# Routed attention followed by a gated MLP: the second maxima step's mask moved beside the scores in 32-row tiles

## The chip, the cores and the metric

The kernel runs on one core of a Trainium2 chip. The metric is the device time of one execution in microseconds (us); lower is better. Before the change the median of three runs is 1022.64 us (1022.56 to 1022.86).

## The reference

```python
B, H, S, D = 4, 8, 768, 64          # 16 clusters
q_assign = argmax(q_n @ c_n.T); k_assign = argmax(k_n @ c_n.T)      # per head, rows normalised
mask = q_assign[:, :, :, None] == k_assign[:, :, None, :]
scores = where(mask, (q @ k.T) / sqrt(D), -1e9)
attn = softmax(scores)               # less the row's maximum, sum + 1e-9
x = (attn @ v) laid out as (B*S, H*D) = (3072, 512)
h = x @ w_in                         # w_in (512, 2048)
g = h * erf(softplus(h))
out = g @ w_out                      # w_out (2048, 512)
```

A query attends only to the keys that chose the same cluster. All inputs are float32.

## The kernel before

**Two stages.** Attention takes the 32 heads in 16 pairs (`NPAIR`), two heads of 64 rows on the 128 partitions. Its result goes through DRAM (`x_dram`) to the second stage, the two large products with the gate between, worked as a seven-product scheme on 2 x 2 blocks (`block`, `hidden`, `project`). The change touches attention; of the second stage it renames one step in a list (`weights`).

**Scores with mask and shift in one accumulation.** A score tile `sc` has keys on the partitions, 128 at a time (`j` = 0 to 5), and 384 queries (`half` = 0, 1) in the columns, with one PSUM bank per head. `products` (line 410) puts q.k into it in float32, two matmuls for each head. `scores` (423) then adds a bfloat16 matmul of `km` and `qm`. In these, a head has 64 rows: the first 16 rows hold the one-hot of the cluster (for queries) or 0 and -2^60 (for keys), so that pairs of different clusters get a large negative number; row 32 (`SH`) holds the shift, the negated maximum of the query, against 1 in `km`. So one matmul adds mask and shift. `curve` (436) takes the exponential on ScalarE, `accumulate` (441) sums on GpSimd, `attend` (453) multiplies by v into a bank `turned[half]`, and `divide` (465) closes a half: TensorE sums the denominators with `minus` into the other `turned` bank, ScalarE takes Ln and Exp of it (`inv`), and VectorE reads the bank again (`den`), scales (`turned<-turned,inv`) and writes `x`.

**Maxima a half ahead.** The shift needs each query's maximum before its exponentials. `maxima_step` (367) computes it from bfloat16 copies `qv`, `kv`: two matmuls of 64 rows (one per head) for q.k into the one tile `wide` (two banks), two for the mask (`qm`, `km`, 64 rows), then one reduction on VectorE (`nmx<-wide`). Twelve such steps serve a pair. After steps 5 and 11 `lowest` is formed, and `turn` (390) transposes it on TensorE and copies it with ScalarE into row 32 of `qm` (`CAST qm<-turned`).

**Routing.** `similarities` (311) multiplies queries and keys by the centroids (four matmuls of 32 columns, in `turned[1]`), `choose` (324) finds the maxima and their one-hots on VectorE (`sims`, `hot`, `hotT`). Rows 0 to 63 of `hotT` belong to the queries, 64 to 127 to the keys, 32 of them for each half. `masks` (350) spreads them with the 0/1 matrix `pick` into a bank (`turned<-hotT,pick`, one matmul of 64 rows), and ScalarE copies the bank to `qm` or, scaled and biased by `nbig`, to `km`.

**Order of work.** Every engine's instructions keep the order of the program (`InOrder`). It is written out in `period(p, i)` (720), called for i = 0 to 5 for every pair p; a period deals with two score tiles, u and u + 1. TensorE's part in order:

- at i = 0 and 3 `turn`; `step_ahead(u)`: one maxima step for half a pair later (711); `mask(0)`;
- at the start of a half, `divide`'s VectorE work (`next(part[0])`);
- `products(u)`, `products(u + 1)`; `mask(1)`; `step_ahead(u + 1)`, the second maxima step;
- `scores(u)`, `scores(u + 1)`; `mask(2)`; at i = 3 the similarities of pair p + 2;
- later in the period `attend(u - 2)`, `attend(u - 1)`, and at i = 0 and 3 `divide`'s matmuls, followed by its Ln and Exp.

`MASKS` (51) says at which i and place the next pair's masks are made: `(0, 1): ("k", 0), (0, 2): ("k", 1), (2, 0): ("q", 0), (5, 0): ("q", 1)`. The bank is `turned[0]` for i = 0 and 5 and `turned[1]` otherwise. ScalarE's order in a period is: turn's copies, `curve(u)`, the copy of place 2's mask, `curve(u + 1)`, then a step of a weight conversion and the casts `kv`, `qv` (i = 4 and 5), then Ln and Exp.

**Conversions of weights.** Pieces of the second stage's weights (128 x 512 float32) are converted beside attention, 22 of them, two per pair: `fetch` (a DMA on SP's queue), `size_and_rest` (two ScalarE activations), `bounded` (VectorE, maximum with 2), `sign` (a ScalarE activation to int16), `shifted` (VectorE), `summed` (GpSimd, followed by the next fetch). Lines 763 to 778 place them, `n1 = 2p - 1` and `n2 = 2p`:

```python
i == 0: shifted(n1 - 1)                  i == 3: shifted(n1); size_and_rest(n2)
i == 1: size_and_rest(n1)                i == 4: sign(n2)
i == 2: bounded(n1); sign(n1)            i == 5: bounded(n2)
# GpSimd: summed(n1 - 1) at i == 1, summed(n1) at i == 4
```

So the last of them are in pair 11. From pair 11 on, `FORMS` places VectorE sums of the weights (`left_forms`) in the periods. `transposes` puts `in_q` of pair p + 2 through VectorE at i = 0, `in_k` at i = 2.

Of the kernel before, what the change touches and what calls it, by code (L numbers as in the profile page):

```python
# [43 lines left out]
BIG = 2.0**60  # L44
FLOOR = 2.0**50
EPS = 2.0**-70
SH = 2 * C
NPT = NJ + 2
N_LATE = 10
LAST_X = 11  # L50
MASKS = {(0, 1): ("k", 0), (0, 2): ("k", 1), (2, 0): ("q", 0), (5, 0): ("q", 1)}
FIRST_MASKS = {(2, 0): ("k", 0), (2, 1): ("q", 0), (2, 2): ("k", 1), (5, 0): ("q", 1)}


# [17 lines left out]
def kernel(  # L72
# [167 lines left out]

    def bounded(n):
        w = w_steps[n][0]
        ve.tensor_scalar(out=w, in0=w, scalar1=2.0, scalar2=None, op0=ALU.max)

    def sign(n):
        hi, _, upper = steps[n]
        ae.activation(out=upper, in_=hi, func=ACT.Prelu, scale=2.0**-25, alpha=2.0**90)

    def shifted(n):
        w = w_steps[n][0].bitcast(U32)  # L250
        ve.tensor_scalar(out=w, in0=w, scalar1=3, scalar2=None, op0=ALU.logical_shift_left)
# [6 lines left out]

    ve.memset(nbig, 0.0)
    for e in range(2):  # L260
        ve.memset(nbig[e * D : e * D + C], -BIG)
        ve.memset(nbig[e * D + SH : e * D + SH + 1], 1.0)
    for t in maxima:
        ve.memset(t, FLOOR)
    ve.memset(pick, 0.0)
# [45 lines left out]
    def similarities(p):  # L311

        if p >= NPAIR:
            return
        st = pairs[p]
        st["psim"] = turned[1][:, 0:HW]
        for g in range(4):
            te.matmul(
                st["psim"][2 * C * g : 2 * C * (g + 1)], lhsT=ccT[:, p % HP],
                rhs=st["qk"[g // 2] + "T"][:, (g % 2) * HW : (g % 2 + 1) * HW],  # L320
                start=True, stop=True,
            )

# [23 lines left out]
        if p < NPAIR:  # L347
            ae.copy(out=pairs[p][nm + "v"], in_=pairs[p][nm + "T"])

    def masks(p, nm, half, bank):  # L350

        if p >= NPAIR:
            return lambda: None
        st = pairs[p]
        cols = slice(half * HW, (half + 1) * HW)
        r = slice(0, D) if nm == "q" else slice(D, P)
        won = bank[:, 0:HW]
        te.matmul(won, lhsT=pick[r, half], rhs=st["hotT"][r], start=True, stop=True)
        if nm == "q":
            return lambda: ae.activation(out=st["qm"][:, cols], in_=won, func=ACT.Relu)  # L360
        return lambda: ae.activation(
            out=st["km"][:, cols], in_=won, func=ACT.Identity, bias=nbig, scale=BIG
        )

    turns = []

    def maxima_step(p, i, sm=wide):

        st = pairs[p]
        nmx = maxima[p % 2]  # L370
        t, half = divmod(i, 2)
        for a, b, start in (("qv", "kv", True), ("qm", "km", False)):
            for e in range(2):
                r = slice(e * D, (e + 1) * D)
                te.matmul(
                    sm[:, e, 0:HW], lhsT=st[a][r, t * P : (t + 1) * P],
                    rhs=st[b][r, half * HW : (half + 1) * HW], start=start, stop=not start,
                )
        ve.tensor_reduce(
            out=nmx[:, :, t, half], in_=sm[:, :, 0:HW], axis=AX.X, op=ALU.max, negate=True  # L380
        )
        if i in (NJ - 1, 2 * NJ - 1):
            h = i // NJ
            ve.tensor_reduce(
                out=lowest[h][:, :, SH::D].rearrange("p t e -> p e t"),
                in_=nmx[:, :, h * HJ : (h + 1) * HJ], axis=AX.X, op=ALU.min,
            )
            turns.append((p, h))

    def turn(p, h, copies=(ae.copy, ae.copy)):  # L390

        st = pairs[p]
        pn = turned[h][:, 0:HW].rearrange("p (t n) -> p t n", t=HJ)
        for t in range(HJ):
            for e in range(2):
                cols = slice(e * D, (e + 1) * D)
                te.matmul(pn[cols, t], lhsT=lowest[h][:, t, cols], rhs=identb, start=True, stop=True)
        for e, copy in zip(range(2), copies):
            r = slice(e * D + SH, e * D + SH + 1)
            copy(out=st["qm"][r, h * HW : (h + 1) * HW], in_=pn[r].rearrange("p t n -> p (t n)"))  # L400
        st["shift", h] = True

# [20 lines left out]
    def scores(u):  # L423

        p, half, j = units[u]
        st = pairs[p]
        sc = sc_of[u]
        assert ("shift", half) in st
        for e in range(2):
            r = slice(e * D, (e + 1) * D)  # L430
            te.matmul(
                sc[:, e, 0:HW], lhsT=st["km"][r, j * P : (j + 1) * P],
                rhs=st["qm"][r, half * HW : (half + 1) * HW], start=False, stop=True,
            )
# [273 lines left out]

    def step_ahead(u):
        p, i = divmod(u + NJ, 2 * NJ)
        if p < NPAIR:
            maxima_step(p, i)

    forms = sum((left_forms(ve, *w_in_parts(f, 2)) for f in range(0, HF, 2)), [])
    routing = [iter(())]
# [2 lines left out]
    def period(p, i):  # L720
        u = 2 * NJ * p + 2 * i
        n1, n2 = 2 * p - 1, 2 * p
        early = lambda n: 0 <= n < N_EARLY

        def mask(place):
            which = (MASKS if p else FIRST_MASKS).get((i, place))
            if which:
                return masks(p + 1, *which, turned[0 if i in (0, 5) else 1])
            return lambda: None

        if u > 0:
            for which in turns if i in (0, 3) else ():
                turn(*which)
                turns.remove(which)
            step_ahead(u)
        mask(0)()
        next(part[0], None)
        if u == 2:
            next(routing[0])
        products(u)  # L740
        products(u + 1)
        mask(1)()
        if u > 0:
            step_ahead(u + 1)
        next(part[0], None)
        scores(u)
        scores(u + 1)
        later = mask(2)
        if i == 3:
            similarities(p + 2)  # L750
            routing[0] = choose(p + 2)
        curve(u)
        later()
        curve(u + 1)
        if u == 0:
            step_ahead(1)
            similarities(1)
            routing[0] = choose(1, turned[0])
            next(routing[0])
            next(routing[0])  # L760
            vectors(1, "q")
            vectors(1, "k")
        if i == 0 and early(n1 - 1):
            shifted(n1 - 1)
        elif i == 1 and early(n1):
            size_and_rest(n1)
        elif i == 2 and early(n1):
            bounded(n1)
            sign(n1)
        elif i == 3:  # L770
            if early(n1):
                shifted(n1)
            if early(n2):
                size_and_rest(n2)
        elif i == 4 and early(n2):
            sign(n2)
        elif i == 5 and early(n2):
            bounded(n2)
        for work in forms[: FORMS.get(p, {}).get(i, 0)]:
            work()  # L780
            forms.remove(work)
        if i == 3:
            for _ in range(3):
                next(routing[0], None)
        if i == 0:
            if p:
                transposes(p + 2, "q")
        elif i == 1:
            load(p + 1, "v", v, vp)
            if p == 0:  # L790
                run(routing[0])
                transposes(2, "q")
        elif i == 2:
            transposes(p + 2, "k")
        elif i == 4:
            vectors(p + 2, "k")
        elif i == 5:
            run(routing[0])
            vectors(p + 2, "q")
        if u > 0:  # L800
            for w in (u - 2, u - 1):
                accumulate(w)
            if i == 1 and early(n1 - 1):
# [32 lines left out]
    vectors(0, "q")  # L836
    vectors(0, "k")
    for r in (0, D):
        for half in range(2):
            for e in range(2):  # L840
                c = r + half * Q + e * C
                ve.tensor_copy(
                    out=pick[r : r + D, half, e * D : e * D + C], in_=first[r : r + D, c : c + C]
                )
    also = ps_s.tile([P, 2, 512], F32, name="sc", tag="s")
    products(0)
# [11 lines left out]
    for n in range(PLACES - 1):  # L858
        fetch(n)
    for i in range(NJ):  # L860
        maxima_step(0, i, also if i % 2 else wide)
# [46 lines left out]

    def weights(n):
        return [  # L910
            functools.partial(w, N_EARLY + n) for w in (size_and_rest, bounded, sign, shifted, summed)
        ]

    def all_weights(lo, hi):
# [76 lines left out]
```

## Time and profile before

| | |
|---|---|
| median of the runs | 1022.64 us |
| profiled execution | 1022.77 us |
| its span, first to last instruction | 1021.1 us |
| granted TensorE clock | 1.00 |
| attention | to about 435 us |
| busy from 43.80 to 307.71 us (pairs 1 to 10) | PE 263.7, VectorE 198.4, ScalarE 210.7, GpSimd 199.1 of 263.9 us |

All work is recorded under line 63, a helper's, so groups are told apart by tiles: `out<-in`. PE is TensorE's matmuls, PEld its weight loads, DVE VectorE, ACT ScalarE, POOL GpSimd. A timeline line has the start (us), the time to the end of the last one merged into it (us), engine, line, operation, tiles, shapes, count, and in brackets the idle time before it and what ended it. `64*128` is a tile of 64 rows by 128 columns. TensorE's matmuls are pipelined and their ends modelled, so two that start together each show their full duration, and distances between starts are what to read. A float32 matmul of 384 columns is recorded as two instructions.

### The profile page before, as it was taken

The page shows a single profiled execution, that of the slowest core. Times are in us where ns is not written, and L with a number is a line of the kernel's source. Part 1 is how long each engine was busy: PE and PEld are TensorE (multiplying, and loading weights), DVE is VectorE, ACT ScalarE, POOL GpSimd, SP SyncE. Part 2 cuts the span into 40 slices and gives each one's busy share as a digit, 9 for nine tenths or more (in the row PEclk, how much of TensorE's full clock was granted, in tenths as well). Part 3 has the DMA queues.
Part 4 walks back from the last instruction along what each step waited for, and adds up shares of the span by engine and source line. Part 5 has one row for each costly group of instructions (what it writes and reads, how often), then busy time and mean ns, then how long its engine had stood idle before and what let it go on. Part 6 is the DMA issues. An engine that isn't in the chain of part 4 may idle for free.

```text
span 1021.1 us, 15464 instructions
## 1 busy us (share of the span) xinstructions
PE 1013.9 (99%) x5930; PEld 726.1 (71%) x5930; DVE 695.8 (68%) x1305; ACT 515.0 (50%) x673; POOL 345.7 (34%) x229
## 2 busy tenths in 40 slices
PE   8999999999999999999999999999999999999998
PEld 3555555554555445478888888888888888888887
DVE  8777777777777777778875674756565547565754
ACT  3787877787777666567615142322233141505050
POOL 1777777777777667745130000000000000000000
PEclk9999999999999999999999999999999999999999
DMA  9344444444343311041100100110011000000001
GB/s 214 68 98 97 104 104 103 104 104 104 83 104 87 76 28 32 24 154 61 42 1 21 63 1 1 42 42 1 1 41 42 1 21 22 1 1 21 21 1 41
DMA packets 141641, 55.55 MB, mean 54 GB/s; under 512 B 127104, under 2 KB 131456, under 8 KB 141568
## 3 DMA queue, kind: packets, MB, share of 16 engines
q1 hardware_dynamic: 139216, 54.28, 20.8%
q8 instruction: 46, 0.75, 0.3%
q10 hardware_dynamic: 2352, 0.30, 0.2%
q14 instruction: 27, 0.22, 0.1%
HBM read 41.98 MB, written 12.58 MB: 53 GB/s over the span
## 4 chain that ended last, share of the span: by engine, by line
PE 97%; DVE 1%; POOL 0%; ACT 0%; issue 0%; DVEq 0%; ACTq 0%; POOLq 0%
PE bank L63 43%; PE turned L63 33%; PE sc L63 15%; PE wide L63 7%; DVE nmx L63 1%; POOL more_out L63 0%; DVE sims L63 0%; ACT inv L63 0%; DVE kT L63 0%; DVE qT L63 0%; ACT pr L63 0%; DVE hotT L63 0%; DVE wide L63 0%; DVE den L63 0%; DVE hot L63 0%
## 5 line engine op out<-in xcount | busy, mean ns | idle before, releaser
L63 POOL TENSOR_TENSOR more_out<-more_out,pr 128x768 f32<-128x768 f32 x128 | 223.5, 1746 | 67.6 <-ACT pr L63 62.5
L63 DVE TENSOR_REDUCE nmx<-wide 128x2 f32<-128x768 f32 x189 | 180.7, 956 | 95.1 <-PE wide L63 70.8
L63 ACT ACTIVATE pr<-sc 128x768 f32<-128x768 f32 x192 | 147.0, 810 | 75.0 <-PE sc L63 75.0
L63 PE MATMUL turned<-pr,in_v 128*64 128x386 f32 x768 | 145.5, 500 | 0.1
L63 DVE TENSOR_TENSOR g<-bank,g 128x256 f32<-128x256 f32 x222 | 89.5, 421 | 52.9 <-PE bank L63 46.3
L63 PE MATMUL bank<-x_own,w_in 128*128 128x256 f32 x424 | 104.5, 380 | 0.0
L63 PE MATMUL bank<-w_out,g 128*128 128x256 f32 x448 | 103.1, 379 | 0.0
L63 PE MATMUL sc<-qT,kT 64*128 64x384 f32 x528 | 99.7, 484 | 0.0
L63 PEld LDWEIGHTS turned<-pr,in_v 128*64 128x64 f32 x768 | 46.7, 136 | 72.2 <-issue 71.1
L63 PEld LDWEIGHTS bank<-w_out,g 128*128 128x128 f32 x448 | 85.2, 190 | 11.5
L63 PEld LDWEIGHTS bank<-x_own,w_in 128*128 128x128 f32 x424 | 80.4, 190 | 12.1 <-issue 1.2
L63 ACT COPY g<-bank 128x256 f32<-128x256 f32 x28 | 10.4, 372 | 152.5 <-PE bank L63 148.5
L63 DVE TENSOR_TENSOR osb<-bank,osb 128x256 f32<-128x256 f32 x87 | 35.4, 420 | 72.8 <-ACT osb L63 25.4
L63 ACT ACT_TABLE_LOAD x48 | 61.6, 1283 | 45.7 <-DVE g L63 45.0
L63 POOL TENSOR_TENSOR more_out<-pr,pr 128x768 f32<-128x768 f32 x32 | 58.8, 1837 | 58.5 <-ACT pr L63 58.5
L63 PE MATMUL bank<-x_more,more_in 128*128 128x256 f32 x296 | 76.0, 379 | 0.0
L63 PEld LDWEIGHTS <-qv 64*128 64x128 bf16 x384 | 25.6, 93 | 65.2 <-issue 51.1
L63 PE MATMUL wide<-kv,qv 64*128 64x384 bf16 x378 | 69.4, 328 | 1.1 <-ACT km L63 0.6
L63 PEld LDWEIGHTS sc<-qT,kT 64*128 64x128 f32 x528 | 56.6, 187 | 16.6 <-issue 1.2
L63 PE MATMUL wide<-km,qm 64*128 64x384 bf16 x378 | 68.3, 322 | 0.0
L63 PE MATMUL bank<-more_out,g_more 128*128 128x256 f32 x272 | 64.3, 379 | 0.0
L63 DVE TENSOR_TENSOR g<-a_s,g 128x512 f32<-128x512 f32 x96 | 62.4, 688 | 1.4 <-ACT a_s L63 1.4
(162 smaller groups left out, 1710.2 us busy)
## 6 DMA issues: line engine op xcount, KB each, us to landing
x_own<-in_moe_w_in_dram SPq DMA_DIRECT2D x13, 512.0 KB, 4.3
in_v<-in_v_dram SPq DMA_DIRECT2D x32, 192.0 KB, 2.9
x_dram<-more_out SPq DMA_DIRECT2D x32, 192.0 KB, 2.4
x_own<-x_dram SPq DMA_DIRECT2D x6, 1024.0 KB, 5.1
out_dram<-osb SPq DMA_DIRECT2D x23, 256.0 KB, 2.0
in_k<-in_k_dram SPq DMA_DIRECT2D x59, 96.0 KB, 2.7
in_q<-in_q_dram SPq DMA_DIRECT2D x58, 96.0 KB, 3.6
g_more<-in_moe_w_out_dram SPq DMA_DIRECT2D x6, 512.0 KB, 3.6
```

What stands on the lines that cost most here:

```text
L63: ins = getattr(self.engine, name)(*args, **kw)
```

## The change

The rows are laid out anew. `hotT` now has, for each half, 32 rows of queries and 32 of keys. `pick` and `nbig` are set so that a bank of masks has two copies in a head's 64 rows: rows 0 to 31 with the shift's row as row 0, and rows 32 to 63 without a shift. `scores` uses the first 32 rows of a head alone. The second maxima step of a period is split: q.k first, then `scores(u)`, then the mask from rows 32 to 63 of each head, then `scores(u + 1)`. The first step of a period still uses 64 rows. Masks at place 2 (`place > 1`) are made from 32 rows of `hotT`, and `MASKS` has the keys' masks at `(0, 2)` and `(2, 2)`. `bounded` in attention becomes a `tensor_tensor` maximum whose second operand is one PSUM column of `wide`, set to 2 at the start and broadcast; after attention the old form stays, as `bounded_late`. The places of `sign` and `size_and_rest` change. `similarities` goes through its four matmuls in another order.

```diff
-SH = 2 * C
-MASKS = {(0, 1): ("k", 0), (0, 2): ("k", 1), (2, 0): ("q", 0), (5, 0): ("q", 1)}
+MASKS = {(0, 2): ("k", 0), (2, 0): ("q", 0), (2, 2): ("k", 1), (5, 0): ("q", 1)}
...
     def bounded(n):
         w = w_steps[n][0]
+        ve.tensor_tensor(out=w, in0=w, in1=lower_bound.to_broadcast([P, LC]), op=ALU.max)
+
+    def bounded_late(n):
+        w = w_steps[n][0]
         ve.tensor_scalar(out=w, in0=w, scalar1=2.0, scalar2=None, op0=ALU.max)
...
-        ve.memset(nbig[e * D : e * D + C], -BIG)
-        ve.memset(nbig[e * D + SH : e * D + SH + 1], 1.0)
+        for n in range(2):
+            r = e * D + n * Q
+            ve.memset(nbig[r : r + C + 1], -BIG)
+            ve.memset(nbig[r : r + 1], 1.0 - n)
+    lower_bound = wide[:, 1, 511:512]
+    ve.memset(lower_bound, 2.0)
...
-                rhs=st["qk"[g // 2] + "T"][:, (g % 2) * HW : (g % 2 + 1) * HW],
+                rhs=st["qk"[g % 2] + "T"][:, (g // 2) * HW : (g // 2 + 1) * HW],
...
-    def masks(p, nm, half, bank):
+    def masks(p, nm, half, bank, narrow=False):
...
-        r = slice(0, D) if nm == "q" else slice(D, P)
+        n = "qk".index(nm)
+        r = slice(half * D + n * Q, half * D + (n + 1) * Q) if narrow else slice(half * D, (half + 1) * D)
         won = bank[:, 0:HW]
-        te.matmul(won, lhsT=pick[r, half], rhs=st["hotT"][r], start=True, stop=True)
+        te.matmul(won, lhsT=pick[r, n], rhs=st["hotT"][r], start=True, stop=True)
...
-    def maxima_step(p, i, sm=wide):
+    def maxima_step(p, i, sm=wide, behind=False):
...
-        for a, b, start in (("qv", "kv", True), ("qm", "km", False)):
+
+        def passes(a, b, start, rows):
             for e in range(2):
-                r = slice(e * D, (e + 1) * D)
+                r = slice(e * D + rows.start, e * D + rows.stop)
                 te.matmul(
                     sm[:, e, 0:HW], lhsT=st[a][r, t * P : (t + 1) * P],
                     rhs=st[b][r, half * HW : (half + 1) * HW], start=start, stop=not start,
                 )
+
+        passes("qv", "kv", True, slice(0, D))
+        if behind:
+            yield
+        passes("qm", "km", False, slice(Q, D) if behind else slice(0, D))
...
     def scores(u):
...
             r = slice(e * D, (e + 1) * D)
+            r = slice(r.start, r.start + Q)
...
-    def step_ahead(u):
+    def step_ahead(u, behind=False):
         p, i = divmod(u + NJ, 2 * NJ)
-        if p < NPAIR:
-            maxima_step(p, i)
+        steps = maxima_step(p, i, behind=behind) if p < NPAIR else iter(())
+        if not behind:
+            run(steps)
+        return steps
...
-                return masks(p + 1, *which, turned[0 if i in (0, 5) else 1])
+                return masks(p + 1, *which, turned[0 if i in (0, 5) else 1], place > 1)
...
-        if u > 0:
-            step_ahead(u + 1)
+        second = step_ahead(u + 1, True) if u > 0 else iter(())
+        next(second, None)
+        scores(u)
+        next(second, None)
         next(part[0], None)
-        scores(u)
         scores(u + 1)
...
         if i == 0 and early(n1 - 1):
             shifted(n1 - 1)
+            sign(n1 - 1)
         elif i == 1 and early(n1):
             size_and_rest(n1)
         elif i == 2 and early(n1):
             bounded(n1)
+        elif i == 3 and early(n1):
+            shifted(n1)
             sign(n1)
-        elif i == 3:
-            if early(n1):
-                shifted(n1)
-            if early(n2):
-                size_and_rest(n2)
         elif i == 4 and early(n2):
-            sign(n2)
+            size_and_rest(n2)
         elif i == 5 and early(n2):
             bounded(n2)
```

Left out of the diff: the setup of `pick`, the rows that `lowest` and `turn` use for the shift (0 and 64 instead of 32 and 96), and `bounded_late` in `weights`.

More of the change, by code (lines that the diff above doesn't have):

```diff
@@ L384, in maxima_step @@
             ve.tensor_reduce(
-                out=lowest[h][:, :, SH::D].rearrange("p t e -> p e t"),
+                out=lowest[h][:, :, ::D].rearrange("p t e -> p e t"),
                 in_=nmx[:, :, h * HJ : (h + 1) * HJ], axis=AX.X, op=ALU.min,
@@ L398, in turn @@
         for e, copy in zip(range(2), copies):
-            r = slice(e * D + SH, e * D + SH + 1)
+            r = slice(e * D, e * D + 1)
             copy(out=st["qm"][r, h * HW : (h + 1) * HW], in_=pn[r].rearrange("p t n -> p (t n)"))
@@ L838 @@
     for r in (0, D):
-        for half in range(2):
+        for n in range(2):
             for e in range(2):
-                c = r + half * Q + e * C
+                c = r + n * Q + e * C
                 ve.tensor_copy(
-                    out=pick[r : r + D, half, e * D : e * D + C], in_=first[r : r + D, c : c + C]
+                    out=pick[r : r + D, n, e * D : (e + 1) * D].rearrange("p (n c) -> p n c", n=2)[:, :, 1 : C + 1],
+                    in_=first[r : r + D, c : c + C].unsqueeze(1).to_broadcast([D, 2, C]),
                 )
@@ L860 @@
     for i in range(NJ):
-        maxima_step(0, i, also if i % 2 else wide)
+        run(maxima_step(0, i, also if i % 2 else wide))
         if i == 1:
@@ L910, in weights @@
         return [
-            functools.partial(w, N_EARLY + n) for w in (size_and_rest, bounded, sign, shifted, summed)
+            functools.partial(w, N_EARLY + n) for w in (size_and_rest, bounded_late, sign, shifted, summed)
         ]
```

## The prediction

> **What bounds the kernel now.** I read the page first: busy shares, then the chain that ended last. Its TensorE lines:
>
> ```profile
> PE 1013.9 (99%) x5930; PEld 726.1 (71%) x5930; DVE 695.8 (68%) x1305; ACT 515.0 (50%) x673; POOL 345.7 (34%) x229
> PE 97%; DVE 1%; POOL 0%; ACT 0%; issue 0%; DVEq 0%; ACTq 0%; POOLq 0%
> ```
>
> TensorE is the chain, so only what adds or removes time on TensorE counts, and a wait on another engine counts where TensorE stands for it. The table of stretches says where such waits are near: over ten pairs of heads, 43.80 to 307.71 us, VectorE is busy 198 of 264 us, ScalarE 211, GpSimd 199.
>
> The change touches only attention (to about 435 us). There I cut the timeline into periods, from one first matmul `wide<-kv,qv` of a period to the next. They repeat in every pair: 4.97, 3.82, 4.15, 5.48, 3.82, 4.15 us for i = 0 to 5 (pair 11: 307.71, 312.68, 316.50, 320.64, 326.12, 329.94, 334.09). One plain period (i = 1), timeline:
>
> ```profile
> 312.68 0.34 PE L63 MATMUL wide<-kv,qv 64*128 64x384 bf16 x2
> 312.86 0.58 ACT L63 ACTIVATE inv<-turned,alleps 128x384 f32<-128x384 f32 x1 [0.62 <-PE turned L63]
> 313.47 0.52 ACT L63 ACTIVATE inv<-inv 128x384 f32<-128x384 f32 x1
> 314.10 0.55 DVE L63 SCALAR_TENSOR_TENSOR den<-turned,inv 128x384 f32<-128x384 f32 x1
> 314.31 0.33 PE L63 MATMUL wide<-kv,qv 64*128 64x384 bf16 x2
> 314.47 0.33 PE L63 MATMUL wide<-km,qm 64*128 64x384 bf16 x2
> 314.63 0.49 PE L63 MATMUL sc<-qm,km 64*128 64x384 bf16 x4
> 315.05 1.52 PE L63 MATMUL turned<-pr,in_v 128*64 128x386 f32 x8
> 316.50 0.34 PE L63 MATMUL wide<-kv,qv 64*128 64x384 bf16 x2
> ```
>
> Durations on PE overlap; starts are the price. Two 64-row matmuls together take a slot of 0.16 (314.31 to 314.47 to 314.63). Four `sc<-qm,km` are two slots, 0.32, yet the next line starts after 0.42: the 0.10 more is the change from 64-row tiles to 128 rows by 64 columns. A change of the rows alone is in the preamble:
>
> ```profile
> 14.20 0.33 PE L63 MATMUL wide<-km,qm 64*128 64x384 bf16 x2
> 14.46 0.50 PE L63 MATMUL turned<-lowest,identb 128*128 128x384 bf16 x2
> 14.88 0.34 PE L63 MATMUL sc<-kv,qv 64*128 64x384 bf16 x2
> ```
>
> One slot plus 0.10 one way, two slots of 0.16 plus 0.10 back.
>
> **The change, part by part.** (us; the sum is made against the profiled execution, 1022.77 with a span of 1021.1; the median shown, 1022.64, is 0.13 lower.)
>
> 1. *The second step's mask beside scores(u).* Takes away one slot, 0.16, and adds a change from 64-row to 32-row tiles. No row shows 64 to 32; bounds are 0.00 (adjacent matmuls of one shape: no extra) and 0.15 (the change to `turned<-pr,in_v`, 0.10 and its first slot 0.05 longer). I take 0.10, what all the row changes above cost. That four tiles of 32 rows share a slot is not shown either; nearest is the four column tiles of `turned<-qT,ccT`, which start within 0.02 of each other at 323.25, and the two row tiles of every line above. Saved: 0.06 in each of 92 periods (1 to 92 have a second step): **-5.5** (bounds -14.7 and -0.9). Periods 0 and 93 to 95 have only the change of tile: 4 x 0.10 = **+0.4**.
>
> The Trainium skill speaks against this part twice. TensorEngine Tiling (Array Packing), Key Properties: going to another tiling mode, not merely another tile, drains TensorE; that covers the case 64 to 32 that no row here shows. TensorE: Matmul & The Clock Gate, "Measured speedup vs the span model": four row tiles gave 3.07 times, not 4. By that an estimated 4/3.07 x 0.16 = 0.21 for the slot would make this part 92 x 0.05 = 4.6 dearer.
>
> 2. *The keys' masks.* Before, both are in i = 0, in one bank, and the second waits for ScalarE to read the first:
>
> ```profile
> 309.35 0.32 PE L63 MATMUL turned<-hotT,pick 64*128 64x384 bf16 x1
> 309.71 0.58 ACT L63 ACTIVATE km<-turned,nbig 128x384 bf16<-128x384 f32 x1 [0.41 <-PE turned L63]
> 310.25 0.81 ACT L63 ACTIVATE pr<-sc 128x768 f32<-128x768 f32 x1
> 310.34 0.32 PE L63 MATMUL turned<-hotT,pick 64*128 64x384 bf16 x1
> 310.96 0.58 ACT L63 ACTIVATE km<-turned,nbig 128x384 bf16<-128x384 f32 x1
> 311.42 0.81 ACT L63 ACTIVATE pr<-sc 128x768 f32<-128x768 f32 x1
> ```
>
> Pair 15 prepares no next pair, and its i = 0 takes 4.46 (411.98 to 416.44) against 4.97: 0.51 for the two. Afterwards each is a third tile beside scores(u+1), one in i = 0 and one in i = 2, in tiles of the size already set. In i = 2 its bank holds the queries' mask until ScalarE has read it (318.08), 0.6 before it is due. So **-7.1** for pairs 1 to 14, and -0.16 for the one of pair 0. If they took slots of their own, it would be 2 x 0.16 x 14 = 4.5 less.
>
> 3. *sign off i = 2.* In i = 3 scores(u) waits for the copies `qm<-turned`, which stand behind the 1.36 of sign on ScalarE (320.44, copies 321.82 to 322.78, matmul 322.84). Pair 12, without weights, has 5.36, of which 0.09 is another wait (part 4). So 5.48 - 5.27 = 0.21, 11 pairs: **-2.3**. The mask copy that comes to i = 2 (0.46 from start to start) still leaves the copies done 0.7 before they are due.
>
> 4. *bounded as tensor_tensor with a PSUM operand.* `w_in<-w_in` TENSOR_SCALAR takes 417 ns. The like of the new one is `hot<-sims,wide`, PSUM broadcast too: 553 ns for 384 elements; `g<-bank,g` takes 421 for 256, so 132 more for each 128, and 0.69 for 512: +0.27. In i = 5 the chain on VectorE grows by that, by 0.10 (the masks come after the change of tile) and by 0.06 (shorter period), against 0.38 idle (at 308.25): the reduction comes 0.05 late, which the 0.13 from its end to the second `wide<-kv,qv` (314.18 to 314.31) takes; 0.5 in all if not. In i = 2 kT's transposition and the next reduction follow, and pair 12 shows it, with a form in bounded's place:
>
> ```profile
> 346.29 0.68 DVE L63 TENSOR_TENSOR w_in<-w_in 128x512 f32<-128x512 f32 x1
> 346.88 0.97 DVE L63 STREAM_TRANSPOSE more_out<-in_k 128x768 f32<-128x768 f32 x1
> 347.78 0.92 DVE L63 TENSOR_REDUCE nmx<-wide 128x2 f32<-128x768 f32 x1
> 348.75 0.34 PE L63 MATMUL wide<-kv,qv 64*128 64x384 bf16 x2
> ```
>
> The second `wide<-kv,qv` is due 1.63 after the period's start (347.03), at 348.66, and starts at 348.75: 0.09 late, because `wide` is read until 348.70. After the change the masked maxima come 0.10 later and the period ends 0.06 earlier: 0.25 late in pairs 1 to 11, 0.16 more than now in pairs 12 and 13. **+3.1** (0 to 4.5, with 0.41 a pair at most). Gains for GpSimd from the other form I put at nothing: its sums are not waited for.
>
> 5. *ScalarE in i = 0.* Here sign arrives and one `km` copy leaves. Queued behind sign are divide's Ln and Exp, behind them VectorE's den, and for den waits the next period's `turned<-pr,in_v`, which overwrites the bank. From the start of i = 0: the curve at 2.32 (2.38 in the fence from 312.68 to the curve at 315.06, 0.06 earlier), copy +0.71, curve +0.46, sign +0.71, Ln +1.09 (sign at 303.52, next start 304.61), Exp +0.61, its end +0.52: 6.42; den from 6.48 to 7.03. The period lasts 4.97 - 0.51 - 0.06 = 4.40, so den ends 2.63 into i = 1, where the matmul is due at 2.37 - 0.06 = 2.31. With 0.06 for the handing over 0.38 late, 11 pairs: **+4.2** (0 if something starts earlier; 0.68, 7.5, if Ln starts 1.38 after sign, as the copy at 321.82 does). In i = 3 sign replaces two activations of 0.57 each from start to start: no change, and Ln there had 0.32 idle. size_and_rest in i = 4 replaces sign: the same. sign is still done before GpSimd's summed in i = 1, which keeps its place with its fetch on SP's queue.
>
> 6. Similarities in another order, nbig, the setup of pick, bounded_late after attention: as many instructions of the same kind, 0.
>
> Sum: -5.5 + 0.4 - 7.1 - 0.2 - 2.3 + 3.1 + 4.2 = **-7.4**; 1022.77 - 7.4 = 1015.4, and 1015.3 against the median. I predict **1015.4**.
>
> **Rivals.**
> - *The new waits don't show* (parts 4 and 5 at 0): 1015.4 - 7.3 = 1008.1. For it: both are differences of 0.25 to 0.4 between chains of 5 us. Against: pair 12 shows the one already. Chance 0.18.
> - *The change of tile is dearer or Ln later*: at 0.15 instead of 0.10, +4.6 + 0.2; Ln late by 0.68, +3.3: 1020 to 1023.5. For it: four sets of weights must be loaded behind the drain rather than two. Chance 0.18.
> - *Slower: tiles of 32 rows do not share a slot*, so the change doesn't do what it says. Place: scores(u) and the mask, 96 periods. Then no slot is saved and the change of tile is paid: +9.6; the keys' masks give 7.1 - 4.5 = 2.6; -0.2 becomes 0; with -2.3 + 3.1 + 4.2 that is +12.0: 1034.8. It decides from a shared slot of 0.16 + 7.4/92 = 0.24. For it: no row of the trace shows four row tiles at once. Against: two row tiles and four column tiles share without loss. Chance 0.13.
>
> **Numbers.** Forecast 1011 to 1019.5: 0.51. A difference under 0.2% (2 us) is about what a measurement of this kernel cannot tell from none. Faster, under 1020.6: 0.51 + 0.18 + 0.04 of the dear case = 0.73; the rest of that, 0.14, same; slower 0.13. The range leaves out the slower rival and takes in the others: from 1006 (part 1 at its bound of -14.7 with the waits kept is 1006.2) to 1023.5.
>
> **What would show it.** Right: scores(u) and `wide<-km,qm` as four starts within 0.02, 0.26 after the second `wide<-kv,qv`; period 4 and 5 at 3.76 and 4.09; i = 0 at 4.40; i = 1 longer than 3.76 in pairs 1 to 11 and 3.76 from 12 on, its `turned<-pr,in_v` waiting for den; i = 3 at 5.46, late at its second `wide<-kv,qv`. Wrong: `wide<-km,qm` 0.16 behind scores(u), more than 0.30 between `wide<-kv,qv` and scores(u), or i = 1 at 3.76 everywhere.

## The result and the profile after

The changed kernel takes 1030.03 us (median of six, 1029.69 to 1031.63) against 1022.76 for the kernel before on the same chip (six, 1022.56 to 1022.86): a ratio of 1.0076 (95% interval 1.0063 to 1.0089), **slower by 7.3 us**. The forecast was 1015.4, faster by 7.4, with a range to 1023.5. Two of the six took 1.6 us more at a mean granted clock of 0.998; the profiled one is one of these (1031.63, span 1029.9), and in it TensorE's clock falls once, in pair 13.

The page of after, the busy shares and the engines of the chain:

```profile
PE 1009.3 (98%) x5930; PEld 705.8 (69%) x5930; DVE 711.1 (69%) x1310; ACT 508.4 (49%) x673; POOL 340.6 (33%) x229
PE 79%; DVE 10%; ACT 3%; DMA 2%; POOL 2%; issue 2%; SPq 1%; DVEq 0%; POOLq 0%
```

TensorE was 97% of the chain and is 79% now, VectorE has 10%, and VectorE's busy time rose from 695.8 to 711.1 us. TensorE has as many instructions as before, so it has begun to wait for VectorE.

I cut both timelines into the same periods, from one first `wide<-kv,qv` to the next. Lengths in us:

| | i = 0 | 1 | 2 | 3 | 4 | 5 | pair |
|---|---|---|---|---|---|---|---|
| before, pairs 2 to 11 | 4.97 | 3.82 | 4.15 | 5.48 | 3.82 | 4.15 | 26.39 |
| forecast | 4.40 | 4.14 | 4.09 | 5.46 | 3.76 | 4.09 | 25.94 |
| after, pairs 2 to 10 | 4.57 | 3.97 | 4.34 | 5.47 | 3.76 | 4.28 | 26.39 |
| before, pair 12 | 4.97 | 3.82 | 4.15 | 5.36 | 3.82 | 4.15 | 26.27 |
| after, pair 12 | 5.93 | 3.76 | 4.11 | 6.92 | 3.76 | 4.09 | 28.57 |

Attention begins 0.4 us later than before (first period at 20.59 instead of 20.16) and pair 12 at 334.22 instead of 334.09: up to there only 0.3 us is won. Attention ends at 445.47 instead of 436.62, and the rest takes 584.44 in both. **The whole loss is in the last four pairs**, in i = 0 and i = 3: 5.93 and 6.92 in pair 12, 5.92 and 8.61 in pair 13 (the clock; in the two runs below with `bounded` alone changed it is 6.92), 5.92 and 5.27 in pair 14, 5.29 in pair 15.

The shared slots are there. The timeline of after in i = 1 of pair 11, the answer to the first fence of the prediction:

```profile
314.21 0.33 PE L62 MATMUL wide<-kv,qv 64*128 64x384 bf16 x2
...
314.47 0.34 PE L62 MATMUL sc<-qm,km 32*128 32x384 bf16 x2
...
314.48 0.34 PE L62 MATMUL wide<-km,qm 32*128 32x384 bf16 x2
...
314.64 0.32 PE L62 MATMUL sc<-qm,km 32*128 32x384 bf16 x2
...
315.11 0.20 PEld L62 LDWEIGHTS turned<-pr,in_v 128*64 128x64 f32 x4 [0.54 <-DVE den L62]
```

Four 32-row matmuls start within 0.01 us, 0.26 behind the second `wide<-kv,qv`, and scores(u + 1) follow 0.17 behind them. The last line is the forecast wait for `den`. It is not all: after, the end of i = 5 in pair 10 and the start of i = 0 in pair 11:

```profile
307.29 0.68 DVE L62 TENSOR_TENSOR w_out<-w_out,wide 128x512 f32<-128x512 f32 x1
...
307.83 0.28 PEld L62 LDWEIGHTS <-qv 64*128 64x128 bf16 x2
...
308.01 0.34 PE L62 MATMUL wide<-kv,qv 64*128 64x384 bf16 x2
...
310.07 0.32 PE L62 MATMUL sc<-qm,km 32*128 32x384 bf16 x2
310.08 0.32 PE L62 MATMUL turned<-hotT,pick 32*128 32x384 bf16 x1
```

The last two lines: a keys' mask shares a slot with scores(u + 1), 0.01 apart. But the weights of `wide<-kv,qv` are loaded from 307.83 and the matmul starts only at 308.01, 0.04 after `bounded` (307.29 + 0.68) has ended. `bounded` reads the column of 2s at the end of `wide`, into which this matmul writes other columns. Both heads' matmuls start only then, although head 0's, which comes first, writes the first of `wide`'s two banks and the column lies in the second (`wide[:, 1, 511:512]`): what waits here goes by the tile `wide`, not by the one bank.

`hot` holds the same tile once more, at the end of i = 3. After, pair 11, from the end of i = 2 to the start of i = 4:

```profile
320.17 0.68 DVE L62 TENSOR_TENSOR w_out<-w_out,wide 128x512 f32<-128x512 f32 x1
...
320.77 0.97 DVE L62 STREAM_TRANSPOSE kT<-in_k 128x768 f32<-128x768 f32 x1
...
320.90 0.34 PE L62 MATMUL wide<-kv,qv 64*128 64x384 bf16 x2
...
321.66 0.92 DVE L62 TENSOR_REDUCE nmx<-wide 128x2 f32<-128x768 f32 x1
...
322.63 0.34 PE L62 MATMUL wide<-kv,qv 64*128 64x384 bf16 x2
...
325.76 0.55 DVE L62 TENSOR_TENSOR hot<-sims,wide 128x384 bf16<-128x384 f32 x1
...
326.21 0.26 PEld L62 LDWEIGHTS <-qv 64*128 64x128 bf16 x2 [0.60 <-issue]
...
326.37 0.34 PE L62 MATMUL wide<-kv,qv 64*128 64x384 bf16 x2
```

The second `wide<-kv,qv` starts 1.73 after the first (320.90 to 322.63) instead of 1.63, behind the reduction: 0.10 late. The first one of i = 4 has its weights at 326.21 and starts at 326.37, 0.06 after `hot` has ended: 0.16 late. Both are so in pairs 2 to 11.

And the form (one of the VectorE sums of the weights that `FORMS` places) in pair 12, which the prediction's fence at 346.29 shows for before. Before, one line was left out there, GpSimd's sum of exponentials:

```profile
346.38 3.88 POOL L63 TENSOR_TENSOR more_out<-more_out,pr 128x768 f32<-128x768 f32 x2 [0.56 <-ACT pr L63]
```

It starts 0.09 **behind** the form (346.29, 0.68). The same place after:

```profile
347.34 3.77 POOL L62 TENSOR_TENSOR more_out<-more_out,pr 128x768 f32<-128x768 f32 x2 [0.49 <-ACT pr L62]
...
347.45 2.12 DVE L62 TENSOR_TENSOR w_in<-w_in 128x512 f32<-128x512 f32 x1
...
350.39 0.92 DVE L62 TENSOR_REDUCE nmx<-wide 128x2 f32<-128x768 f32 x1
...
351.36 0.34 PE L62 MATMUL wide<-kv,qv 64*128 64x384 bf16 x2 [1.55 <-DVE nmx L62]
```

Here the sum starts 0.11 **ahead** of the form, and the form takes 2.12 instead of 0.68. The reduction behind it is late, and TensorE waits 1.55. The same turn, from 0.09 or 0.10 ahead to 0.11 behind, is seen in all eight forms in i = 2 and 5 from pair 11's i = 5 to pair 15's i = 2. TensorE's waits from 330 to 440 us, in total, count and longest; before has no such row:

```profile
PE wide L62 <- DVE nmx L62: 8.0, 7, 1.6
```

### The profile page after: what moved, and what is told of

It is laid out like the page before. It is cut to its first block, busy times and chain, and to the rows that moved or that the text cites. A ratio compares the mean times of both kernels' runs of the same rounds, so it can differ in the third digit from the quotient of the medians.

```text
span 1029.9 us, 15459 instructions
## 1 busy us (share of the span) xinstructions
PE 1009.3 (98%) x5930; PEld 705.8 (69%) x5930; DVE 711.1 (69%) x1310; ACT 508.4 (49%) x673; POOL 340.6 (33%) x229
## 4 chain that ended last, share of the span: by engine, by line
PE 79%; DVE 10%; ACT 3%; DMA 2%; POOL 2%; issue 2%; SPq 1%; DVEq 0%; POOLq 0%
PE bank L62 42%; PE turned L62 22%; PE sc L62 11%; PE wide L62 5%; DVE nmx L62 4%; POOL more_out L62 2%; ACT pr L62 1%; DMA in_q<-in_q_dram 1%; DVE w_in L62 1%; DVE more_in L62 1%; DMA x_dram<-more_out 1%; DVE sims L62 1%; DVE wide L62 1%; DVE hot L62 1%; ACT x_own L62 1%
## 5 line engine op out<-in xcount | busy, mean ns | idle before, releaser
L62 POOL TENSOR_TENSOR more_out<-more_out,pr 128x768 f32<-128x768 f32 x128 | 218.6, 1708 | 67.5 <-ACT pr L62 62.3
L62 PEld LDWEIGHTS <-qv 64*128 64x128 bf16 x384 | 28.9, 93 | 80.8 <-issue 65.5
L62 PE MATMUL wide<-kv,qv 64*128 64x384 bf16 x378 | 66.8, 327 | 12.5 <-DVE nmx L62 8.4
L62 PE MATMUL wide<-km,qm 64*128 64x384 bf16 (+1 forms) x378 | 62.9, 327 | 0.0
```

Source lines behind the costliest of these rows:

```text
L62: ins = getattr(self.engine, name)(*args, **kw)
```

## The experiments

Three theories for the 14.6 us between forecast and result. **ORDER**: a VectorE instruction that reads two tensors in SBUF stands until a running sum of GpSimd's has ended, if the sum began first; the change turned this order in the late pairs. **BANK**: `bounded` with its PSUM operand holds TensorE's next `wide<-kv,qv`. **ROWS**: the new rows themselves, the shared slot and the change of tile, cost more than was forecast. Each run was timed beside the kernel before, which gave 1022.6 to 1022.8 each time.

**bounded in its old form**, the rest of the change kept.

```diff
-        ve.tensor_tensor(out=w, in0=w, in1=lower_bound.to_broadcast([P, LC]), op=ALU.max)
+        ve.tensor_scalar(out=w, in0=w, scalar1=2.0, scalar2=None, op0=ALU.max)
```

> The changed kernel with bounded in its old form (tensor_scalar, one SBUF operand and a constant) at its new place. Theory ORDER: a VectorE instruction that uses both of its SBUF reads and starts after a GpSimd sum has started stands until that sum ends (forms at i = 2 and 5 took 2.12 us instead of 0.68 where they start 0.11 after GpSimd's sum, and 0.68 where they started 0.09 before). The old bounded would start 0.11 after too, twice a pair, and stand some 1.3 us each: 11 pairs x 2 x 1.2 = 26, about 1055 us. Theory BANK (PSUM column in wide's bank keeps the next wide<-kv,qv waiting, 0.44 a pair) without ORDER: the wait is gone, 4.8 less: 1025 us. Rival ROWS (the mask behind the scores makes the reductions too late by itself): 0.27 x 11 less on VectorE, 1027 us.

Measured: 1050.6, ratio 1.0271 (1.0256 to 1.0286). Its timeline at the start of i = 3 of pair 2:

```profile
83.38 3.50 POOL L62 TENSOR_TENSOR more_out<-more_out,pr 128x768 f32<-128x768 f32 x2 [0.75 <-ACT pr L62]
...
83.49 1.85 DVE L62 TENSOR_SCALAR w_in<-w_in 128x512 f32<-128x512 f32 x1
...
87.13 0.34 PE L62 MATMUL wide<-kv,qv 64*128 64x384 bf16 x2 [1.29 <-DVE nmx L62]
```

The old form, 0.42 in before, now begins 0.11 after the sum and takes 1.85; i = 3 grows from 5.47 to 6.81. So not only two SBUF operands but this tensor_scalar too stands behind GpSimd, and the PSUM operand is what spares `bounded` this (in after it takes 0.68 at 307.29, 0.11 behind a sum that began at 307.18). BANK's local part shows as well: i = 5 falls from 4.28 to 4.09 and i = 2 from 4.34 to 4.17.

**GpSimd's sum a little later**: a copy of four columns on GpSimd ahead of it, from pair 11 on.

```diff
+            if p > 10 and i % HJ == 0:
+                ge.tensor_copy(out=probe, in_=prs[(u - 2) % NPT][:, 0, 0:4])
```

> The changed kernel with one small GpSimd copy (128x4, of the same exponentials) ahead of the sums of periods i = 0 and 3 from pair 11 on, so that GpSimd's sum starts some 0.1 to 0.3 us later and the form of VectorE first. ORDER: the forms take 0.68 again, seven periods lose 1.3 to 1.5 us each, 9.3 in all: 1020.7 us (1019 to 1023), although work is added. BANK and ROWS: nothing changes but the small instruction: 1030 us.

Measured: 1031.79, ratio 1.0092 (1.0077 to 1.0107), a miss that decides nothing: the copy moved the sum by 0.06 alone, the form still began 0.05 after it and took 2.18. The new tile also moved the first period to 21.84, 1.25 later.

**Forms moved** to places where they do not meet the sum (their number is kept).

```diff
-    11: {5: 1}, 12: {0: 1, 2: 1, 5: 1}, 13: {0: 1, 2: 1, 5: 1}, 14: {0: 2, 2: 1, 3: 1, 5: 1},
-    15: {0: 1, 2: 1, 3: 2, 4: 2, 5: 2},
+    12: {0: 1, 3: 1}, 13: {0: 1, 3: 1}, 14: {0: 2, 3: 2}, 15: {0: 2, 2: 2, 3: 2, 4: 3, 5: 3},
```

> The changed kernel with the VectorE sums of the weights (forms) placed at i = 0 and 3 of pairs 12 to 14, where GpSimd has no sum when they start, instead of i = 2 and 5. ORDER: i = 0 and 3 of pairs 12 to 15 return to 4.40 and about 5.3: 9.3 less, 1020.7 us. ROWS: the same time as the changed kernel, 1030 us, since the number of VectorE instructions is the same.

Measured: 1022.60, ratio 0.9997 (0.9988 to 1.0007): 7.4 of the 9.3 us that the late pairs lose against the forecast come back by the order of VectorE's work alone. Pair 12 has 4.57 and 5.62 for i = 0 and 3, instead of 5.93 and 6.92; pair 14 has 4.41 for i = 3.

**bounded moved** to i = 3 and 0, in its old form, away from the `wide<-kv,qv` that waited for it.

```diff
+            bounded(n1 - 1)
             shifted(n1 - 1)
...
-        elif i == 2 and early(n1):
-            bounded(n1)
         elif i == 3 and early(n1):
+            bounded(n1)
             shifted(n1)
...
-        elif i == 5 and early(n2):
-            bounded(n2)
```

> The changed kernel with bounded in its old form and at i = 3 and 0, ahead of shifted, where GpSimd has no sum when it starts; no PSUM column is read. BANK: the next period's wide<-kv,qv no longer waits behind i = 2 and 5 (0.25 and 0.19), the reduction of i = 3 is no longer 0.25 late: 0.65 x 11 = 7 less, 1023 us. Without BANK only the late reduction of i = 3 goes: 0.25 x 11 = 2.7 less, 1027.3 us. The forms keep costing 9.3.

Measured: 1030.07, ratio 1.0072 (1.0055 to 1.0089). The two waits go (i = 5 from 4.28 to 4.09, i = 2 from 4.34 to 4.17), which is 0.36 a pair, and i = 3 takes 5.81 instead of 5.47. There `bounded` stands ahead of the routing, and `sims` and `hot` are late: `minus` writes the bank that `sims` reads and starts 0.28 later than in the kernel with the waits removed (4.72 against 4.44 after the period's start), and `hot`, which reads `wide`, now holds the next `wide<-kv,qv` by 0.30 instead of after's 0.16. The waits of this run from 40 to 330 us have a row for it, which after's do not have:

```profile
PE wide L62 <- DVE hot L62: 2.5, 11, 0.2
```

The gain was given back in the same pair; the forecast for this run had looked at the place that bounded leaves and not at what stands behind it where it goes.

**Both moved**, forms and bounded (the two diffs above).

> Forms and bounded both moved to i = 0 and 3, bounded in its old form, rows as changed. ORDER and BANK together: 1030.0 - 9.3 - 7 = 1013.7 us (1011 to 1016). If one of the two is wrong, 1020 to 1023. ROWS: 1027 to 1030.

Measured: 1022.62, ratio 0.9999 (0.9990 to 1.0009): as for the forms alone, with the periods 4.57, 3.97, 4.17, 5.81, 3.76, 4.09. The miss is that of the run before it.

**The second step's mask in a slot of its own**, with 64 rows, on the kernel with both moved.

```diff
-        second = step_ahead(u + 1, True) if u > 0 else iter(())
-        next(second, None)
+        if u > 0:
+            step_ahead(u + 1)
         scores(u)
-        next(second, None)
```

> As the kernel with forms and bounded moved, but the second step's mask in 64 rows and in its own slot ahead of scores(u), as before the change; scores still in 32-row tiles, so the change of tile stays. If four 32-row tiles share one slot, a slot of 0.16 comes back in 92 periods: 14.7 more than the kernel with both moved, about 1028.5 us. If the shared slot saves nothing, the same time.

Measured: 1031.83, ratio 1.0089 (1.0074 to 1.0104), 9.2 above the kernel with both moved, where 14.7 was to come from 92 slots of 0.16. The periods are 4.73, 3.97, 4.33, 5.64, 3.92, 4.25: 0.16 more in i = 0, 2, 4 and 5, nothing in i = 1, where `den` is waited for anyway, and 0.17 less in i = 3, where there was a wait for `hot`. The slot is worth its 0.16 wherever no wait hides it. ROWS falls.

**The old rows with the new places** of forms, bounded, sign and size_and_rest, made from the kernel before.

```diff
+            bounded(n1 - 1)
             shifted(n1 - 1)
+            sign(n1 - 1)
...
-        elif i == 2 and early(n1):
+        elif i == 3 and early(n1):
             bounded(n1)
+            shifted(n1)
             sign(n1)
...
-            sign(n2)
+            size_and_rest(n2)
```

> The kernel before the change (64-row masks and scores, the keys' masks at i = 0) with the forms, bounded, sign and size_and_rest placed as in the kernel with both moved. What is left between the two is the layout of the rows with the keys' masks: by the prediction 5.5 - 0.4 + 7.3 = 12.4 us, of which the shared slots 5.5 and the keys' masks 7.3. So 12.4 more than the kernel with both moved, about 1026. If the rows are worth nothing, the same time as with both moved.

Measured: 1026.24, ratio 1.0035 (1.0022 to 1.0049), with periods 4.97, 3.82, 4.15, 5.64, 3.82, 4.15. So in these places the new rows are worth 3.6 us, not 12.4. Unhidden they would give 0.51 + 6 x 0.06 = 0.87 a pair; 26.55 - 26.37 = 0.18 is left in each of pairs 1 to 11, and the waits in i = 0 to 3 of the two kernels take the other 0.69 (by difference, not read wait by wait).

**Before, with a copy ahead of its forms**: 128 x 4 elements, to bring the form behind the sum.

```diff
+        if p > 10 and i in (2, 5):
+            ve.tensor_copy(out=probe, in_=probe)
```

> The kernel before the change with one small VectorE copy (128x4) ahead of the forms of i = 2 and 5 from pair 11 on. ORDER: the forms then start after GpSimd's sum, which follows them by 0.09 now, and stand 1.4 us each; 7 of them on the path: about 10 us slower, 1032 us, for seven instructions of some 0.1 to 0.2. ROWS and BANK: 1023 to 1024 us.

Measured: 1025.97, ratio 1.0038 (1.0024 to 1.0052). Short of the expectation: in the late pairs the form still began 0.03 ahead of the sum. But in pair 11 the copy came behind it; the timeline of this run:

```profile
321.43 3.62 POOL L63 TENSOR_TENSOR more_out<-more_out,pr 128x768 f32<-128x768 f32 x2 [0.53 <-ACT pr L63]
...
321.67 1.65 DVE L63 COPY probe<-probe 128x4 f32<-128x4 f32 x1
```

Four columns take 1.65 us, and 0.16 in pair 12, where no sum runs when they start: what is paid is the rest of the sum, not work. That i = 3 has 6.65. The new tile made the preamble 1.4 longer.

**Waits removed**: both moved, and besides bounded, shifted and the forms behind the routing's VectorE work in i = 3, sign behind Ln and Exp in i = 0, and `km`'s copy ahead of both curves in i = 0.

```diff
+        if i == 0:
+            later()
...
-        later()
+        if i:
+            later()
...
-            sign(n1 - 1)
...
-            shifted(n1)
...
+            if early(n1):
+                bounded(n1)
+                shifted(n1)
...
+            if i == 0 and early(n1 - 1):
+                sign(n1 - 1)
```

> The kernel with forms and bounded moved, and the four waits that its trace shows taken away: bounded, shifted and the forms of i = 3 go behind the routing's VectorE work (there `hot`, which reads a PSUM column in wide's bank, held the next wide<-kv,qv by 0.23); sign of i = 0 goes behind Ln and Exp (den held turned<-pr,in_v by 0.21, and through x the mask of i = 2 by 0.08); at i = 0 ScalarE copies the keys' mask ahead of both curves (that copy held the minus matmuls by 0.11). If the rows are worth what the prediction said and only such waits ate it, a pair takes 4.42 + 3.76 + 4.09 + 5.25 + 3.76 + 4.09 = 25.4 against 26.4: 1011 us (1009 to 1013). If the shared slots were worth less, 1018 to 1022.

Measured: **1017.85**, ratio 0.9952 (0.9937 to 0.9967), 4.8 us faster than the kernel before and the fastest of all. The periods are 4.41, 3.76, 4.10, 5.19, 4.39, 4.09: as forecast without the waits, or below, in all but i = 4. Its timeline there, in pair 8:

```profile
242.18 1.84 POOL L61 TENSOR_TENSOR more_out<-pr,pr 128x768 f32<-128x768 f32 x1 [0.93 <-DVE sims L61]
...
243.24 1.53 DVE L61 TENSOR_SCALAR w_in<-w_in 128x512 f32<-128x512 f32 x2
```

`bounded` and `shifted` (0.88 for both where no sum runs) met the next sum: ORDER again. The second `wide<-kv,qv` of i = 4 waits 0.46 for the reduction behind them, and the period is 0.63 too long; 11 x 0.63 = 6.9 is the whole distance from 1017.85 to the 1011 expected.

**The sum split**: the changed kernel as it is, with GpSimd's first sum of i = 0 and 3 from pair 11 on made in two, 16 columns of each head and then 368. VectorE's program is untouched.

```diff
-            ge.tensor_tensor(out=acc, in0=so_far, in1=pr[:, :, 0:HW], op=ALU.add)
+            for lo, hi in ((0, 16), (16, HW)) if split else ((0, HW),):
+                ge.tensor_tensor(
+                    out=acc[:, :, lo:hi], in0=so_far[:, :, lo:hi], in1=pr[:, :, lo:hi], op=ALU.add
+                )
...
-                accumulate(w)
+                accumulate(w, p > 10 and i % HJ == 0 and w == u - 2)
```

> The changed kernel with GpSimd's first sum of i = 0 and 3 cut in two from pair 11 on, the first part 16 of 384 columns for each head. ORDER: a form waits only for the short part, some 0.2, and goes ahead of the long one; the 7 forms on the path take about 0.9 instead of 2.12: 8 to 9 less than the changed kernel, 1021 to 1022 us. ROWS: 1030 us or a little more.

Measured: 1021.52, ratio 0.9987 (0.9978 to 0.9997): 8.5 us less than the changed kernel, for some ten **additional** instructions. Its timeline in pair 12:

```profile
346.09 4.03 POOL L62 TENSOR_TENSOR more_out<-more_out,pr 128x32 f32<-128x32 f32 x3 [0.49 <-ACT pr L62]
...
346.20 0.68 DVE L62 TENSOR_TENSOR w_in<-w_in 128x512 f32<-128x512 f32 x1
...
348.67 0.34 PE L62 MATMUL wide<-kv,qv 64*128 64x384 bf16 x2
```

The form still begins 0.11 after GpSimd's first instruction, but that one is short (done 0.13 after the form's start), and the long one comes behind the form. The form takes 0.68, and TensorE's wait of 1.55 is gone. Of the three theories only ORDER fits this.

**Before, with the form later**: four memsets of one column ahead of the forms, pairs 12 to 15, no new tile. No work of the change is in this kernel.

```diff
+        if p > 11 and i in (2, 5):
+            for _ in range(4):
+                ve.memset(alleps, S * EPS)
```

> The kernel before the change with four VectorE memsets of one column (no reads) ahead of the forms of i = 2 and 5 in pairs 12 to 15, some 0.25 in all. ORDER: the forms then start after GpSimd's sum instead of 0.09 before it and stand 1.4 longer; six are on the path, four with about 1.5 and two with 0.9: 7 us slower, 1030 us. Otherwise 0.25 on VectorE beside other work: 1022.7 to 1023.5 us.

Measured: 1029.74, ratio 1.0068 (1.0053 to 1.0083): about the changed kernel's time, by moving the forms 0.4 us (in pair 12 from 3.41 to 3.81 after the start of i = 2). Its timeline in pair 12:

```profile
346.20 3.76 POOL L63 TENSOR_TENSOR more_out<-more_out,pr 128x768 f32<-128x768 f32 x2 [0.55 <-ACT pr L63]
...
346.52 1.91 DVE L63 TENSOR_TENSOR w_in<-w_in 128x512 f32<-128x512 f32 x1
...
350.22 0.34 PE L63 MATMUL wide<-kv,qv 64*128 64x384 bf16 x2 [1.58 <-DVE nmx L63]
```

The form line has its end at 348.43, 0.55 after the first of the two sums merged in the line above ends (346.20 + 1.68 = 347.88); in after the same distance is 349.57 - 349.02 = 0.55. TensorE waits 1.58, and pair 12's i = 3 takes 7.00 instead of 5.36.

**The routing's maxima in another bank**: the kernel with both moved, sign last and `km` first in i = 0, and the maxima that `hot` reads in columns 488 to 511 of `turned[0]` instead of `wide`'s bank.

```diff
-            routing[0] = choose(p + 2)
+            routing[0] = choose(p + 2, turned[0])
```

> Changes to the kernel with forms and bounded moved: sign of i = 0 behind Ln and Exp, the keys' mask copied ahead of both curves at i = 0, and the routing's maxima (the PSUM operand of `hot`) in turned[0] instead of wide's bank, so that bounded, shifted and forms can stay ahead of the routing at i = 3, before GpSimd's sum starts there, without holding wide<-kv,qv. The kernel with the four waits removed lost 0.63 in i = 4 of 11 pairs because bounded and shifted, behind the routing, started after that sum and took 1.53 instead of 0.88. ORDER and BANK with the rows worth what the prediction said: i = 4 back to 3.76, 0.63 x 11 + 0.44 x 2 = 7.8 less, 1010 us (1008.5 to 1012.5). If the maxima's bank makes another wait (attend writes turned[0] until then): up to 0.7 a pair, 1018 us.

Measured: 1056.3, ratio 1.0329 (1.0311 to 1.0346), a miss: the place chosen was a bad one. It has the longest of the waits that BANK speaks of. Its timeline:

```profile
295.00 1.94 PE L61 MATMUL turned<-pr,in_v 128*64 128x386 f32 x8 [2.65 <-DVE hot L61]
```

`turned<-pr,in_v` writes columns 0 to 385 of the bank and waits 2.65 for `hot` to read columns 488 and above; i = 3 grows to 7.7 to 9.2. The wait moved from one bank's next matmul to the other's.

## Why the prediction was wrong, step by step

- *What bounds the kernel*: right that only TensorE's time counts. The table of busy times (VectorE 198 of 264 us) said nothing of one engine that stands while another works.
- *Part 1, the shared slot*: right. The change from 64 to 32 rows takes 0.26 - 0.16 = 0.10 (314.21 to 314.47) as taken, and the slot is worth 0.16 (the run with the mask by itself). The Trainium skill, TensorEngine Tiling (Array Packing), Key Properties, has the drain without a price; 0.10 is what it costs here. The 3.07-fold gain of four row tiles in TensorE: Matmul & The Clock Gate, "Measured speedup vs the span model", measured there with 512 columns, is not seen here with 384: the next slot begins after 0.17, not the estimated 0.21.
- *Part 2, the keys' masks*: right; they cost no slot (310.07 and 310.08). `km`'s copy between the curves does hold `minus` in i = 0: 4.57 instead of 4.40, also in the late pairs where no sign is, and 4.41 with the copy first. In pairs 1 to 11 this is hidden, as the next item says.
- *Part 3, sign off i = 2, with part 4's late reduction in i = 3*: 5.46 forecast and 5.47 measured, but the agreement is luck. Of the 0.25 for the late reduction only 0.10 is seen in i = 3, because i = 2 before it is already 0.25 too long, and `hot`, which was not forecast, adds 0.16.
- *Part 5, den*: right in sum, wrong in place. i = 0 and i = 1 together were forecast at 4.40 + 4.14 = 8.54 and take 4.57 + 3.97 = 8.54, because both end with the same `den`; without the two waits they take 4.41 + 3.76, which is 0.37 a pair or 4.1 us for the +4.2.
- *Part 4, bounded with a PSUM operand*: duration right (0.69 forecast, 0.68 measured). **The step that failed is that only VectorE's chain was followed.** Its operand lies in the tile that the next `wide<-kv,qv` writes, and that matmul waits for it: 0.19 in i = 5 and 0.17 in i = 2. The other 0.08 in i = 2 is the half's late end on VectorE: `x` is done at 316.92, and the queries' mask, which goes into its bank, begins at 316.97. In sum 0.44 a pair, 4.8 us over the eleven pairs. By these lengths alone the 0.17 in i = 2 is not yet a gain to be had: VectorE goes from `bounded` through the transposition to the reduction without a pause (320.17 to 322.58), and TensorE would meet that reduction in i = 3 all the later. Over i = 2 and 3 together, 9.81 against 9.55 forecast, the excess is `hot`'s 0.16 and 0.10 more; no run took away one of these waits alone. The same bank in the Trainium skill: PSUM — Partial Sum Buffer, "PSUM bank collisions raise a hardware error", asks for a guard by bank and quadrant, not by address. The program has such waits, as these rows show; what the chip would do without them no run here shows.
- *Part 4's "Gains for GpSimd from the other form I put at nothing: its sums are not waited for"*: the reason was wrong, though this term cost the forecast nothing. I had asked who waits for GpSimd's sums, not who stands behind them. In before `bounded` starts 0.10 ahead of a sum (319.90 and 320.00), in after 0.11 behind one, and its PSUM operand, which I had priced as 0.27 of pure cost, is what keeps it from standing (1050.6 without it).
- *Part 4's forms in the late pairs*: **the 9.3 us, and the step that turned the sign of the result.** Here the same oversight was dear. The prediction took pair 12's form as an instruction of 0.68 and gave it "0.16 more than now". But its margin was 0.09: the masks behind the scores bring the second reduction, and the form behind it, later by 0.10, the shorter period brings the curve, and the sum that waits for it, earlier by 0.06, and 0.16 is more than 0.09. (Measured in pair 12, from the start of i = 2: the form at 3.54 instead of 3.41, the sum at 3.43 instead of 3.50, together 0.20.) The forecast had both numbers, added them for the reduction, and never set them against GpSimd's line, which stood next to the form in the same timeline and was left out of the fence. Seven periods pay: 3 x (5.93 - 4.40) + 2 x (6.92 - 5.46) + (5.27 - 4.40) + (5.29 - 4.40) = 9.3, of which 3 x 0.17 = 0.5 is `km`'s copy in pairs 12 to 14 and 8.8 the order (the split sum gave 8.5 back). The rule is in the Trainium skill, SBUF — State Buffer, "Who interferes with whom": a VectorE instruction with two SBUF inputs, or a copy or tensor_scalar in a two-port mode, and a GpSimd instruction that reads SBUF exclude each other, and whichever issues second stands still. The runs agree (0.68 to 2.12, 0.42 to 1.85, four columns 0.16 to 1.65).
- *The sum*: 4.8 + 9.3 + 0.5 (a preamble 0.4 later, and rounding) = 14.6 = 1030.0 - 1015.4.
- *The rivals*: neither the dearer change of tile nor the lack of a shared slot was seen. The case without the new waits, 1008.1, is nearly what the kernel with the waits removed reaches outside i = 4 (1017.85 - 6.9 = 1010.9). The slower rival ended on the right side by the wrong mechanism: the one that decided was not among them, and the range took in no turn of an order between two engines.

What stays open: the loss of clock in two of six executions of the changed kernel (also in one of four of the run with GpSimd's sum later and two of five of before with a copy, all at 0.998), and why a tile of four columns makes the preamble 1.25 to 1.4 longer.

## What to carry over

Where VectorE and GpSimd work side by side, list for each VectorE instruction with two SBUF operands (copies and tensor_scalar too) how far its start is from GpSimd's next one; a margin of 0.1 us is a cliff, 0.68 to 2.12 here, and a change that moves both sides by less than that can cost more than it saves. In this kernel an operand in PSUM bought freedom from this and paid with the tile it lies in: the next matmul into other columns of that tile waited for the reader. Moving an instruction is priced by what stands behind it in the new place, as the runs with bounded moved and with the waits removed both showed.

## What was not expected of the hardware

- Three kinds of VectorE instruction stood behind GpSimd's running sum, whatever their own size: 512 columns with two SBUF operands 0.68 to 2.12, tensor_scalar 0.42 to 1.85, a copy of 4 columns 0.16 to 1.65. With one PSUM operand (`bounded`, 0.68) it did not, 0.11 after a sum's start, nor did the small reduction `lowest<-nmx` (0.18 in after at 347.36, 0.02 after a sum's start). If VectorE's begins first, the sum pays: 2.12 to its end behind the form (in before, from 346.38) instead of 1.68.
- The granted clock fell after a short idle time: in after, 1.00 from 372 to 380 us and 0.72 from 380 to 386, behind a wait of 1.55 (379.91), so that i = 3 of pair 13 takes 8.61 instead of 6.92. Another wait of 1.55 in the same execution (351.36) did not do it. In the run with the maxima in another bank, with a wait of 2.65 in each pair, the mean clock is 0.99.
- Four memsets of one column, placed ahead of the forms of four pairs, cost 7 us. Their own busy time is 0.06 each.
